# Attention and a gated FFN on one core: the last group's output projection as seven block products, with all tasks in a new order

## The chip, the cores and the metric

One Trainium2 chip; the kernel uses one of its cores. The metric is the device time of one execution in microseconds (us), less is better. Three timed runs of the kernel before took 246.59, 245.79 and 246.05 us; the median is 246.05 us.

The engines are named as in the profile: PE (TensorE, matrix products; PEld is its weight load), DVE (VectorE), ACT (ScalarE), POOL (GpSimd) and SP (SyncE, which here only issues DMAs). Each has its own queue of instructions, in program order, and waits on semaphores for the others.

## The reference

Causal attention over 4 batches, 8 heads, 768 positions and 64 elements per head; heads 0, 2 and 6 see all earlier positions, the others only the first 4 and the last 64. The result, 3072 tokens by 512, goes through a gated FFN of width 1536.

```python
scores = np.where(mask, q @ k.T / 8, -1e9)        # per batch and head
a = softmax(scores) @ v
x = a.transpose(0, 2, 1, 3).reshape(3072, 512)
g = x @ w_gate
return ((g * sigmoid(g)) * (x @ w_val)) @ w_out
```

## The kernel before

The 24 tiles of 128 tokens are taken in pairs. For each pair q, k and v are loaded, cast to 16 bits and turned (by PE for the first five pairs, by DMA after that). For each tile, score products go to PSUM (L567), ACT takes the exponential (L579), DVE or POOL multiplies masks in (L587), PE forms the values (L597), and DVE divides by the sum (L604, L605). The normalized tile is turned into `xt`, for the first eight tiles by PE and after that by a DMA transpose that SP issues (L615).

Four tiles make a group of 512 tokens, six groups in all. For each group `g` and each of twelve column blocks `j`, there are two blocks of four matmuls of 512 columns: the gate product and the value product (both L759; tasks `gate g.j` and `vals g.j`). ACT takes a tanh of the first (L765), DVE makes `sil` of it (`stt1`, L769), and DVE multiplies by the second into `h_sb` (`stt2`, L775).

The output projection is `h` times `w_out`. For groups 0 to 4 it is done as seven products of half blocks (`seventh`, L839; tasks `out g.p1` to `out g.p7`, 12 matmuls of 256 columns each) in place of eight. Their operands are partly sums of blocks of `w_out` (`ws`, made once, L412), partly sums of blocks of `h` (`hs g.x.part`, L826, on DVE or POOL; `x` 1 to 4, two parts each, one after the other: 1, then 3, then 2, then 4). Sums 2 wait for product 1, which reads the block that they overwrite, and sums 4 for product 2. Product 1 needs the lower half of `h`, products 2 and 4 the upper, product 5 sums 1, product 7 sums 3, product 6 sums 2, product 3 sums 4. The seven results are gathered in `out_sb` (`gathered`, L855, tasks `oe g.name`): `r1` is a copy, the others add a product to a cell. Cells c11, c12, c21 and c22 are the four quarters of the group's result; c12 adds product 3 to r56, which adds product 5 to r67. Two halves of 512 KB are stored per group.

Group 5, the last, is projected directly: per tile twelve matmuls of 512 columns (the last tile 384 and 128), 60 in all (`outproj`, L793). ACT copies the results out, DVE the last 128 columns, and each tile is stored as soon as it is there (L811); the last stores are of 192 and 64 KB.

PSUM has eight banks. Gates, products and scores take a bank each (scores two), and a bank is free when the operation that reads it is done.

The order is not found at run time. Three strings of digits hold it: `ORDER` gives all tasks in one sequence (numbers of 3700 and up are short runs of filling matmuls), `WAYS` the engine for each task that may go to several, `SLOTS` the bank or buffer for each task that takes one. Each engine runs its tasks in the order of that sequence.

Of the kernel before, what the change touches and what calls it, by code (L numbers as in the profile page):

```python
# [7 lines left out]
FP = mybir.dt.float32  # L8
# [8 lines left out]
    "0306071W091U1V1X000A08xy1c0D0C01050B1d1e040gy01f1gzJ1i1h2021282922232B1j1r1s021p1q1w0F2C2D2E2F1b"  # L17
    "2A2L2M2N2O2X2f2g0m1Y1a1Z1t1u1v1k0h252h1l1m2W2c242G2H2I2d2e2l2m2i2j0G271n1o1y1z3C262P2Q2R0z2t3031"
    "2J0y8e8o2n2K102U2o2p3I3J2V8t8j8m8u8v8k8l8n1x2k8f8g8p8q2x382y8h8i118r8s8w8x138y8z9893909495999A33"
    "340n9D9E0E2Z3K3D3L3M3N149B9C9F969G9H972a9192322b2Y2q2r2s2u3R3S3W3X0k1C9c9d9e9h9i9j3U3V3O2z353P36"  # L20
    "39370q1D9f9g9k9l3T3b3i3n3o3f3g0H3H3E3F2v2w0i169I9J9K9N9O9P0o179L9Q9R9M0l1F3Q3Y3Z3c3j3a0I3u40410j"
    "193k3h9m9n9o3l3m3A3B9S9T9U9r9s9t3d3e9X0J3v4344453G3p3q3r0r1G9u9p9v429Y9Z3s3t0x1H2S4647494A4H0p1A"
    "9V9WB74N4O4Q4R0K3z9q9zA10N4c3x4BB4B5B6B8Ak4K4L4V4b4C4D3yAT484M0w0sAQARASAU9a9b9y0t1E0W6K2TAlAmAV"
    "AWAX151M1O1N1PAYAZBEAfAgAhB9BABB4a0u181Q1R1SBCBDAp0v1BBFBGA0AaAbAnAoAc3wBHBIAdAe0L0M0PB20T12A41I"
    "1J1K0S4d4P0O4Z4h4g4Y4e4f5D5L5K0RAzB0B1AqArB31L0YALAM0ZAN4E4F4G4J4I6J1TAuAvAOAPAw9wA2A69xA3A7A55C"
    "5I5JAA4l4m4i4j4kACA8A9ABAD4n4v51524y53AiAj5f5lAEBMAGAFAK4S4z504T4W4UAxAy5g5nAsAtBL4q4r4o4p54BO0c"
    "AHAIAJ4s554t4u4x4wBJBKBQ56575T5U6MBNBP5W5c5XBb5j0X58595A5B707S7T6xBVBW6wBRBS5i5VBXBYBc6z5YBZBaBd"
    "5p5qBT5s605t5u4XBsBtBuCeCbCcCdCfCMCNCOCCBvBwCDCE0V6I5v0Q5F5G5H6v5k5o5M5N5O0UBiBjBk5rCPCQBlBm5E5Z"
    "5a5b5d5wCHCICJCWCXCY5m63696A666768Bh5h73CKCLC7C8C9710eCRCS5P5Q5R6465CACBCTBUC2C36y7Q6P74BnBo5x5y"
    "5z610a72CZCaBp5S625e6H6NBqBrC46B6C6F6D6GCFCGCiBeBfBgBxByBz7O7UC0C1C5C681CUCVCjCl6E6U6V6W6X6Y6R6S"  # L30
    "6T6eDmDjDkDlDnDoDpDqDrDs0b7P7X7WDtDuDv6Z6aCgChCn6b6c6d6fDUDVDWDXDY7576776g7C7D7E7F7G7L0dDwDxCkCm"
    "DSDFDGDHDPDQDRDT7b7c7d6QDADBDCDyDzE0DDDE7H80D5D6D7CsCt6O6n6o6h6i6j6kE1E27V7I7J7M7K7ND8D96l6m7879"
    "7A7BCoCpCrCuCv897Y7Z6p6q8786DKDLDMDZDaDb6L6r6s6t6uDcDdDeDfDgCwCx7e7f7R7j7m7n7o7p7q7rDNDOCyCzD0D4"
    "EhEiEjErEsEcEd88EkElEtCqD1D2D3EuEvEeDhDi7a7g7h7k7iFLFMFNFOFP7x8D8E8A8I8B8C8F8JFJFGFHFIFKFBFCFDDI"
    "DJE5E77s7t8GFEFFEp7u7v7y7w8HEXEYEZ0f838485EmEnEoEqEfEg8NEw8Y8ZE6E88T8U8VEzExEyF0EBE3E9E4EAECEDF6"
    "828K8L8M8OF1F2F3F9EFEG8Q8R8S8W8XEVEHEIEJF7F8FA7l8P7z8a8b8cEaEbESETEUEWEEEOELEM8dGiGMGTGUEKGCENER"
    "G7GVGWGjGkGJGKEPGREQFTFVGXGLGOGPGEGFGNGQG9F4GAGSGGGYGbGZF5GaGcGBGDFSGHFpFqFrFQFRG4G5GdGeFzFUFeFW"
    "FXGIG6G0G8FcFdGfFfFuFvFYFaFbGgGhG1G2G3FsFtFxGlGmFZFwFyFlFiFjFmFnFgFhFkFoGnGoGpGsGtGuGvGwGqGrGxGy"
    "GzH0H2H3H4H5H7H1H6H8H9"
)  # L40
WAYS = (
    "000010000000000000000000000000000000000000000000000000000000221202202202212200200111000111110010"
    "222200001100000000000000220022122022001011000000000000001100212002000011001001000001000001001000"
    "000201021120001000001001000000010010000010000000002221220000000000010000002000100100000020000221"
    "000000000100000002000010010000000000020200000010000000000000110000011000000100100000020001000000"
    "002202200220000000000000000012000100100000000201120000000000000000010002202202010000001001000001"
    "200000000000011002021000000000000000000200000000000000000000000000000000000000000000000000000000"
    "000000000000000000000000000000000000000000001000000000000000000000000000000000000000000000000000"
    "000000000000000000000000000000001000000010000000000000000000000000000000000000000000000000000000"
    "000000000000000000001110100011000000000001000000000000000000000000000000000000000000000000000000"  # L50
    "000000001111000001100000000000100000000000000000000000000000000000000000000000000000000000000111"
    "101100110000000000011000000000000000000000000000000000000000000000000000000000000000010000100000"
    "00000010"
)
SLOTS = (
    "0014237653916A152371476981504A39A2564807049A28352A9168410016041002241601230163620442561014104122"
    "636011642065221025144416322211256461406003404624344620616540610143626540604164236062324342142254"
    "041614064616325426212246140636104325614261306242452460436460636014122636230644521206164434062601"
    "020211341120003102001134000210400214105510131201001011040122021303213020111113411111040020200051"
    "014110101310002114301212131010022102320210013012111032112010000012000102211130011112010111054125"  # L60
# [959 lines left out]
```

## Time and profile before

| what | us |
| --- | --- |
| three timed runs | 245.79, 246.05, 246.59 |
| span of the profiled execution, first to last instruction | 244.4 |
| busy: PE, DVE, ACT, POOL | 234.5, 186.7, 148.5, 129.0 |
| first matmul starts | 1.4 |
| last matmul starts, last copy ends | 241.2, 241.8 |

The profile is of one more execution. Its span runs from the first to the last instruction; of its own whole time only the span is recorded, and the three timed runs lie 1.4 to 2.2 us above it. The profile lists instructions with start and length; the chain of work that ended last is followed back from the last instruction through what released each step. Idle time of an engine that nobody waits for costs nothing.

### The profile page before, as it was taken

To read this page: it belongs to the slowest core of one execution; us is meant where nothing else is said; L and a number is where in the kernel's file an instruction comes from. 1 tells how busy PE (TensorE), PEld (TensorE's weight loads), DVE (VectorE), ACT (ScalarE), POOL (GpSimd) and SP (SyncE) were. 2 spreads that over 40 slices of the span, in tenths; PEclk is the share of its full clock that TensorE was granted. 3 is DMA by queue.
4 is the path that set the end of the run, shared out by engine and by line. 5 is a ranking of instruction groups with operands and counts; after the bars stand their busy time and mean duration, and the time that the engine had idled before them with its cause. 6 is when DMAs were issued, how large, how long until landed. Compare 5 with 4: busy or idle time off the path is not lost.

```text
span 244.4 us, 5604 instructions
## 1 busy us (share of the span) xinstructions
PE 234.5 (96%) x2189; PEld 143.6 (59%) x2189; DVE 186.7 (76%) x324; ACT 148.5 (61%) x235; POOL 129.0 (53%) x140
## 2 busy tenths in 40 slices
PE   7989999998999999799999999999999999999995
PEld 3667855553457678445555457656456764475743
DVE  0577887889999999887987977669769777776800
ACT  3899899887878669487637776563682302330011
POOL 7479999956497552375765446910094110375000
PEclk9999999999999999999999999999999999999999
DMA  6999999999766989999464451519100213100053
GB/s 187 355 348 353 323 352 366 313 362 305 206 131 78 287 165 289 191 268 192 89 130 130 97 120 38 90 36 234 38 4 0 46 21 115 59 0 1 7 203 136
DMA packets 66794, 40.73 MB, mean 167 GB/s; under 512 B 25168, under 2 KB 60240, under 8 KB 66768
## 3 DMA queue, kind: packets, MB, share of 16 engines
q1 hardware_dynamic: 65392, 37.76, 61.5%
q10 hardware_dynamic: 1376, 2.62, 2.9%
q8 instruction: 17, 0.28, 0.5%
q14 instruction: 9, 0.07, 0.1%
HBM read 28.31 MB, written 6.29 MB: 142 GB/s over the span
## 4 chain that ended last, share of the span: by engine, by line
PE 54%; DVE 19%; issue 8%; DMA 6%; POOL 5%; SPq 5%; ACT 2%; DVEq 0%; POOLq 0%
PE banks L759 34%; PE banks L839 10%; PE banks L793 4%; DMA raw<-in_moe_w_val_dram 4%; DVE h_sb L775 4%; PE banks L567 3%; DVE h_sb L826 3%; SPq L349 3%; DVE sil L769 3%; PE banks L597 2%; POOL hs_sb L826 2%; DVE out_sb L855 2%; DVE xb L605 2%; DMA xt<-xb 2%; DVE e L587 2%
## 5 line engine op out<-in xcount | busy, mean ns | idle before, releaser
L759 PE MATMUL banks<-xt,wg_sb 128*128 128x512 f16 (+1 forms) x304 | 70.3, 368 | 1.9 <-DMA xt<-xb 1.4
L759 PE MATMUL banks<-xt,wv_sb 128*128 128x512 f16 (+1 forms) x304 | 70.4, 368 | 0.8 <-DVE sil L769 0.7
L579 ACT ACTIVATE e<-banks 128x1024 f16<-128x1024 f32 (+2 forms) x68 | 58.7, 910 | 20.0 <-PE banks L567 11.7
L765 ACT ACTIVATE sig<-banks 128x512 f32<-128x512 f32 (+1 forms) x76 | 43.0, 577 | 43.5 <-PE banks L759 37.5
L769 DVE SCALAR_TENSOR_TENSOR sil<-sig,banks 128x512 f32<-128x512 f32 (+1 forms) x76 | 49.0, 656 | 14.8 <-ACT sig L765 12.6
L775 DVE SCALAR_TENSOR_TENSOR h_sb<-sil,banks 128x512 f16<-128x512 f32 (+1 forms) x76 | 48.7, 656 | 6.7 <-PE banks L759 4.4
L587 POOL TENSOR_TENSOR e<-e,m 128x640 f16<-128x640 f16 (+1 forms) x22 | 37.8, 1727 | 27.2 <-ACT e L579 24.3
L759 PEld LDWEIGHTS <-wg_sb 128*128 128x128 f16 x304 | 28.5, 98 | 30.7 <-issue 3.1
L759 PEld LDWEIGHTS <-wv_sb 128*128 128x128 f16 x304 | 28.2, 98 | 29.5 <-issue 1.2
L839 PEld LDWEIGHTS <-h_sb 128*128 128x128 f16 x360 | 34.8, 98 | 7.9 <-issue 0.7
L826 POOL TENSOR_TENSOR hs_sb<-h_sb 128x768 f16<-128x768 f16 x7 | 11.5, 1640 | 40.9 <-DVE h_sb L775 29.4
L855 DVE TENSOR_TENSOR out_sb<-banks,out_sb 128x512 f32<-128x512 f32 x35 | 23.6, 685 | 4.7 <-PE banks L839 4.4
L826 POOL TENSOR_TENSOR h_sb<-h_sb 128x768 f16<-128x768 f16 x11 | 18.0, 1639 | 8.2 <-PE banks L839 4.4
L839 PE MATMUL banks<-wo_sb,h_sb 128*128 128x256 f16 x180 | 21.9, 273 | 0.0
L839 PE MATMUL banks<-wt_sb,h_sb 128*128 128x256 f16 x180 | 21.5, 273 | 0.4 <-DVE out_sb L855 0.4
L567 PE MATMUL banks<-qT,kT 64*128 64x128 f16 x472 | 20.6, 218 | 1.1 <-DVE xb L605 1.0
L567 PEld LDWEIGHTS <-kT 64*128 64x128 f16 x472 | 14.6, 94 | 11.0 <-issue 10.2
L597 PEld LDWEIGHTS <-e 128*128 128x128 f16 x472 | 17.1, 97 | 4.3 <-ACT vt L206 0.9
L597 PE MATMUL banks<-vt,e 128*128 128x65 f16 x472 | 18.2, 193 | 1.0 <-POOL vt L208 0.7
L605 DVE TENSOR_TENSOR xb<-banks,rc 128x512 f16<-128x512 f32 x24 | 16.6, 691 | 0.8
L208 POOL CAST vt<-raw 64x512 f16<-64x512 f32 x22 | 14.4, 654 | 4.8 <-DMA raw<-in_v_dram 2.3
L206 ACT COPY out_sb<-banks 128x512 f32<-128x512 f32 (+1 forms) x7 | 4.0, 570 | 19.1 <-PE banks L793 16.0
(60 smaller groups left out, 216.3 us busy)
## 6 DMA issues: line engine op xcount, KB each, us to landing
raw<-in_v_dram SPq DMA_DIRECT2D x12, 512.0 KB, 7.0
raw<-in_q_dram SPq DMA_DIRECT2D x8, 512.0 KB, 4.8
raw<-in_k_dram SPq DMA_DIRECT2D x8, 512.0 KB, 5.1
raw<-in_moe_w_gate_dram SPq DMA_DIRECT2D x6, 512.0 KB, 8.9
raw<-in_moe_w_val_dram SPq DMA_DIRECT2D x6, 512.0 KB, 8.4
raw<-in_moe_w_out_dram SPq DMA_DIRECT2D x6, 512.0 KB, 7.9
out_dram<-out_sb SPq DMA_DIRECT2D x6, 512.0 KB, 4.7
raw<-in_q_dram SPq DMA_DIRECT2D x8, 256.0 KB, 6.4
```

The source lines that it names most:

```text
L567: nc.tensor.matmul(sc[:, c:c + n, :], weights, moving, start=first, stop=last)
L579: nc.scalar.activation(out=to, in_=src, func=AF.Exp, scale=scale)
L587: ENG[task().way].tensor_tensor(out=ev, in0=ev, in1=mm, op=ALU.mult)
L597: nc.tensor.matmul(avs[t][:, odd, n * 66:n * 66 + 65], ee, vv, start=(m == 0), stop=(m == len(bl) - 1))
L605: nc.vector.tensor_tensor(out=xb.rearrange("p n o d -> p o n d"), in0=av[:, :, :, 0:64], in1=rc.to_broadcast([128, 2, 4, 64]), op=ALU.mult)
L759: nc.tensor.matmul(ps, wsb[:, kk, j * 128:(j + 1) * 128], xt[:, kk, c[0]:c[1]], start=(kk == 0), stop=(kk == 3))
L765: nc.scalar.activation(out=sg[g, j, c], in_=gs[g, j, c], func=AF.Tanh, scale=0.5)
L769: nc.vector.scalar_tensor_tensor(out=sl[g, j, c], in0=sg.pop((g, j, c)), scalar=1.0, op0=ALU.add, in1=gs.pop((g, j, c)), op1=ALU.mult)
L775: nc.vector.scalar_tensor_tensor(out=hs[g, j][:, c[0]:c[1]], in0=sl.pop((g, j, c)), scalar=0.5, op0=ALU.mult, in1=vs.pop((g, j, c)), op1=A ...
L826: ENG[T_hs[g, x][part].way].tensor_tensor(out=to, in0=a, in1=b, op=op)
L839: nc.tensor.matmul(rooms[g, p][:, x], left[:, j, 128 * x:128 * x + 128], right[:, j], start=(j == 0), stop=(j == NK - 1))
L855: nc.vector.tensor_tensor(out=cell(*to), in0=rooms[g, p], in1=cell(*other), op=ALU.add)
```

## The change

`SEVENS` goes from 5 to 6, so that group 5 is projected by seven products too. Its product 3, whose result is only needed for cell c12, is made in two halves of one token tile each (`p3.0` and `p3.1`, six matmuls each), each with a bank of its own; c12 is gathered by two additions of 256 columns, and stored as two DMAs of 128 KB. The other three quarters are stored by themselves, with 256 KB each (`store_cell`). All three strings are new, so every task of the kernel may stand elsewhere, on another engine or in another bank. The number of filling matmuls stays 21.

```diff
 ORDER = (
-    "0306071W091U1V1X000A08xy1c0D0C01050B1d1e040gy01f1gzJ1i1h2021282922232B1j1r1s021p1q1w0F2C2D2E2F1b"
...
+    "070006xi03090A0804021W1X0D011fy11U1V0C1g1c0B20211d280g1h1i1e222305292B1j0F1r2C1b1p1s2D0m1Y2A2E1q"
...
-    SEVENS = 5
+    SEVENS = 6
...
-    def seventh(g, p):
+    def halves(g, p):
+        return 2 if g == NG - 1 and p == 3 else 1
+
+    def seventh(g, p, part):
...
-        rooms[g, p] = buf("o", [128, 2, HM], FP, "o_ps")
-        for x in range(2):
+        if halves(g, p) == 1:
+            room = rooms[g, p] = buf("o", [128, 2, HM], FP, "o_ps")
+        else:
+            room = rooms[g, p, part] = buf("o", [128, 1, HM], FP, "o_ps")
+        for n, x in enumerate(range(2) if halves(g, p) == 1 else [part]):
             for j in range(NK):
                 nc.tensor.matmul(
-                    rooms[g, p][:, x], left[:, j, 128 * x:128 * x + 128], right[:, j],
+                    room[:, n], left[:, j, 128 * x:128 * x + 128], right[:, j],
                     start=(j == 0), stop=(j == NK - 1))
...
+        if halves(g, p) == 2:
+            nc.vector.tensor_tensor(
+                out=cell(*to)[:, part:part + 1], in0=rooms[g, p, part],
+                in1=cell(*other)[:, part:part + 1], op=ALU.add)
+            return
...
+    def store_cell(g, name, part):
+        x, y = CELLS[name][1]
+        b, i = TILES[FIRST[g] + 2 * x]
+        r0 = b * S + i * 128
+        at = slice(0, 2) if part is None else slice(part, part + 1)
+        eng = nc.scalar if T_st[g, name, part].way == "ACT" else nc.sync
+        eng.dma_start(
+            out=out[r0 + 128 * at.start:r0 + 128 * at.stop, HM * y:HM * y + HM].rearrange(
+                "(s p) n -> p s n", p=128),
+            in_=cell(x, y)[:, at])
...
+        if g == NG - 1:
+            ends = [("c11", None, c11), ("c21", None, c21), ("c22", None, c22)]
+            for part in range(2):
+                p3 = product(3, T_hs[g, 4] + wo, ["o"], part)
+                c12 = gather("c12", [p3, r56], part)
+                P.uses(p3, "o", c12)
+                ends.append(("c12", part, c12))
+            for name, part, done in ends:
+                st = T_st[g, name, part] = P.add(
+                    f"st{g}.{name}" + ("" if part is None else f".{part}"), ["SP", "ACT"],
+                    (lambda name=name, part=part: store_cell(g, name, part)), deps=[done])
+                P.lands(st)
+            return
```

Three places of the new order, each before and after. In these rows L839 and L855 of before are L845 and L866 of after.

DVE at the end of the program, before: the last `stt2` (L775), four gathering additions of group 4, and the copy of the last 128 columns.

```order
L769 SCALAR_TENSOR_TENSOR sil<-sig,banks 128x512
L775 SCALAR_TENSOR_TENSOR h_sb<-sil,banks 128x512
L855 TENSOR_TENSOR out_sb<-banks,out_sb 128x2x256 x4
L208 COPY out_sb<-banks 128x128
```

DVE at the same place, after: from the last `stt1` on, with the sums of group 5 (L826).

```order
L769 SCALAR_TENSOR_TENSOR sil<-sig,banks 128x512
L775 SCALAR_TENSOR_TENSOR h_sb<-sil,banks 128x512
L826 TENSOR_TENSOR hs_sb<-h_sb 128x768
L775 SCALAR_TENSOR_TENSOR h_sb<-sil,banks 128x512 x2
L866 TENSOR_TENSOR out_sb<-banks,out_sb 128x2x256 x2
L826 TENSOR_TENSOR h_sb<-h_sb 128x3x256
L826 TENSOR_TENSOR h_sb<-hs_sb,h_sb 128x3x256 x2
L866 TENSOR_TENSOR out_sb<-banks,out_sb 128x2x256 x6
L859 TENSOR_TENSOR out_sb<-banks,out_sb 128x256 x2
```

Behind the last `stt2` there were four additions and a copy; now there are two additions of group 4, three sums, and eight additions of group 5, in the order c11, r6, r67, c21, c22, r56, c12 first half, c12 second half. POOL, which had nothing of group 5, now makes four of its eight sums: part 0 of sums 3, then part 1 of sums 1, then both parts of sums 4 (part 1 first). On PE the new end is `out4.p4`, then products 2, 1, 7, 6, 4, 5 and the two halves of 3 of group 5.

SP at the end of the program, before: a store of group 3's second half (L861), then three stores of group 5.

```order
L861 DMA out_dram<-out_sb 128x2x512
L811 DMA out_dram<-out_sb 128x512
L811 DMA out_dram<-out_sb 128x384
L811 DMA out_dram<-out_sb 128x128
```

SP at the same place, after.

```order
L883 DMA out_dram<-out_sb 128x2x512 x3
L874 DMA out_dram<-out_sb 128x2x256 x2
L874 DMA out_dram<-out_sb 128x256 x2
```

Both halves of group 4 are now stored from SP (they were on ACT), and behind them c11, c21 and the two halves of c12; c22 is stored from ACT.

PE between the values of tile 11 (L597, the last of group 2's tiles to be ready) and the first gate of group 2 (L759), before: 48 matmuls of four products of group 1 (L839), then 16 of scores (L567); of each run only the first or last rows are shown.

```order
L597 MATMUL banks<-vt_110,e 128x65
L839 LDWEIGHTS h_sb
...
L839 MATMUL banks<-wt_sb,h_sb 128x256
L567 LDWEIGHTS kT_104
...
L567 MATMUL banks<-qT_107,kT_104 128x128
L759 LDWEIGHTS wg_sb
L759 MATMUL banks<-xt,wg_sb 128x512
```

PE at the same place, after: the scores (16 matmuls) stand behind the first product, and 11 more of scores (8 of tile 12, 3 of tile 14) behind the third.

```order
L597 MATMUL banks<-vt_110,e 128x65
L845 LDWEIGHTS h_sb
...
L567 MATMUL banks<-qT_107,kT_104 128x128
L845 LDWEIGHTS h_sb
...
L567 MATMUL banks<-qT_106,kT_104 128x128
L567 LDWEIGHTS kT_104
L567 MATMUL banks<-qT_107,kT_104 128x128
L845 LDWEIGHTS hs_sb
...
L845 MATMUL banks<-wt_sb,hs_sb 128x256
L759 LDWEIGHTS wg_sb
```

Four products still lie between the two, in the order 7, 6, 4, 5 in place of 6, 2, 7, 4 (product 2 stands ahead of tile 11's values now, and product 5 behind them), and the scores in two runs in place of one.

More of the change, by code (lines that the diff above doesn't have):

```diff
@@ L22 @@
[L22 to L36, printed above, removed]
@@ L869, in tasks_of_sevens, with product @@
         upper = [y for j in range(NK, NJ) for y in T_h[j]]
-        def product(p, deps, takes=(), after=()):
-            T_p[g, p] = P.add(f"out{g}.p{p}", ["PE"], (lambda: seventh(g, p)),
-                              deps=deps, takes=takes, after=after)
+        def product(p, deps, takes=(), part=None):
+            T_p[g, p] = P.add(f"out{g}.p{p}" + ("" if part is None else f".{part}"), ["PE"],
+                              (lambda: seventh(g, p, part)), deps=deps, takes=takes)
             return T_p[g, p]
@@ L881, in sums, with gather @@
                     (lambda part=part: hsum(g, x, part)), deps=deps(part)))
-        def gather(name, deps):
+        def gather(name, deps, part=None):
             T_ga[g, name] = P.add(
-                f"oe{g}.{name}", ["DVE"] if CELLS[name][2] else ["ACT", "DVE"],
-                (lambda: gathered(g, name)), deps=deps)
+                f"oe{g}.{name}" + ("" if part is None else f".{part}"),
+                ["DVE"] if CELLS[name][2] else ["ACT", "DVE"],
+                (lambda: gathered(g, name, part)), deps=deps)
             return T_ga[g, name]
```

69 lines of the change are left out of this document (42 added, 27 removed).

## The prediction

> **What bounds the kernel now.** I read the page first, then the chain of work that ended last, then the busy time by stretches.
>
> ```profile
> span 244.4 us, 5604 instructions
> PE 234.5 (96%) x2189; PEld 143.6 (59%) x2189; DVE 186.7 (76%) x324; ACT 148.5 (61%) x235; POOL 129.0 (53%) x140
> ```
>
> PE is busy for 96% of the span; the next engine, DVE, for 76%. A modelled PE share hides small waits, so the chain matters more. Its columns are start, length, engine and line, and a count of merged instructions.
>
> ```profile
> 95.85 0.50 SPq L615
> 96.40 4.70 DMA xt<-xb
> 101.24 5.34 PE banks L759 x24
> ...
> 136.75 0.85 PE banks L567 x24
> ...
> 141.15 0.33 PE banks L567 x8
> ...
> 197.62 2.62 PE banks L839 x24
> 200.24 13.81 PE banks L759 x64
> 214.05 1.31 PE banks L839 x12
> ...
> 227.06 3.93 PE banks L839 x36
> 230.99 10.40 PE banks L793 x60
> 241.47 0.29 DVE out_sb L208
> ```
>
> From 195 us to 241.4 us the chain is PE alone, each piece starting where the one before ends: there the kernel is bound by PE's work and by nothing else. Before that PE loses time here and there; the largest hole, 101.24, waits for a DMA. Three stretches show the other engines beside it (length, then PE, PEld, DVE, ACT and POOL busy, with counts).
>
> ```profile
> 60.00:100.00 40.00, 39.16 (x406) 27.35 (x404) 38.92 (x66) 29.84 (x44) 21.32 (x19) 1.00 0.90 188
> 100.00:196.00 96.00, 93.37 (x874) 54.83 (x875) 76.22 (x130) 57.42 (x91) 47.82 (x42) 1.00 0.52 107
> 196.00:241.50 45.50, 45.38 (x276) 26.31 (x274) 27.60 (x44) 9.88 (x17) 11.40 (x7) 1.00 0.19 67
> ```
>
> DVE is full from 60 to 100 us (38.92 of 40), and has 18 us free in the last 45.5. PE's granted clock is 1.00 in all three, so it enters no term.
>
> The sum is made against this execution: 244.4 us of span, to which the three timed runs add 1.4 to 2.2 us and their median 246.05 adds 1.65. I carry differences over to the median unchanged.
>
> **The change, part by part.**
>
> *Projection of the last group.* 60 matmuls of line 793 took 10.40 us. In their place stand 84 of 256 columns; twelve of those took 1.31 us (214.05), so 84 take 9.17 us. **-1.23 us**, all on PE at a place where only PE counts.
>
> *The end behind the last matmul.* In the new order, DVE has c22 and r56 (both from product 5), then the two halves of c12, behind the last products.
>
> ```profile
> 220.41 1.03 PE L759 MATMUL banks<-xt,wg_sb 128*128 128x512 f16 x4
> ...
> 220.61 0.69 DVE L855 TENSOR_TENSOR out_sb<-banks,out_sb 128x512 f32<-128x512 f32 x1 [2.06 <-PE banks L839]
> ...
> 224.44 0.69 DVE L769 SCALAR_TENSOR_TENSOR sil<-sig,banks 128x512 f32<-128x512 f32 x1
> 225.23 1.29 DVE L775 SCALAR_TENSOR_TENSOR h_sb<-sil,banks 128x512 f16<-128x512 f32 x2
> ```
>
> Here PE turns to its next task at 220.41 and DVE starts at 220.61: 0.20 us from PE to DVE. Two operations that don't need each other take 1.29 us together and 0.69 each: spacing 0.60. One that needs the result just written follows after 0.79 (224.44 to 225.23).
>
> ```profile
> L769 DVE SCALAR_TENSOR_TENSOR sil<-sig,banks 128x256 f32<-128x256 f32 x8 | 3.1, 419 | 1.7 <-ACT sig L765 1.5
> ```
>
> A half cell of 256 columns is not in this trace as an addition; the nearest row has 0.42 us, and the ends are 0.29 (128 columns, at 241.47) and 0.69 (512). I take 0.42. With E the end of PE: product 5 ends at E-1.31, c22 starts at E-1.11, r56 at E-0.51, c12's first half (it reads r56) at E+0.28, the second 0.34 later, and ends at **E+1.04**. Before, the copy starts at 241.47, 0.20 behind PE, and ends at E+0.49. So **+0.55 us**.
>
> *The last store* grows from 64 KB to 128.
>
> ```profile
> out_dram<-out_sb SPq DMA_DIRECT2D x1, 192.0 KB, 1.9
> out_dram<-out_sb SPq DMA_DIRECT2D x1, 64.0 KB, 1.6
> ```
>
> Between 1.6 and 1.9 us: **+0.15 us**, ends 0 and 0.3. The three earlier quarters issue while PE still works or 0.3 us ahead of it; they cost nothing unless SP's queue holds the last one up.
>
> *Does PE stay fed until E?* What hid waits at the end was 10.4 us of work that needed only h. Now products 7, 6 and 3 wait for sums, and these for the last stt2. I follow the new order by hand from group 4's gate 8 on. To the end of the last gate product PE has 27 blocks of 0.86 us and 7 products of 1.31: 32.5 us. DVE has 40 full operations and 8 sums in it.
>
> ```profile
> 203.50 1.28 DVE L769 SCALAR_TENSOR_TENSOR sil<-sig,banks 128x512 f32<-128x512 f32 x2 [1.21 <-ACT sig L765]
> 204.70 0.68 DVE L855 TENSOR_TENSOR out_sb<-banks,out_sb 128x512 f32<-128x512 f32 x1
> 205.30 0.55 DVE L826 TENSOR_TENSOR h_sb<-h_sb 128x768 f16<-128x768 f16 x1
> 205.76 0.68 DVE L775 SCALAR_TENSOR_TENSOR h_sb<-sil,banks 128x512 f16<-128x512 f32 x1
> ```
>
> At 0.60 each, and 0.46 for a sum (205.30 to 205.76), that is 27.7 us: DVE keeps up, with 4.8 us to spare. The last stt2 starts 0.55 us behind the last gate product. During out4.p4, p2 and p1 (3.9 us) the chain behind it runs: stt2 0.69, the sum on POOL 1.64, the next on DVE 0.55; product 7 finds its operand 0.2 us early. The two sums behind p1 (0.20 + 0.46 + 0.55) are ready 0.1 us before product 7's 1.31 us are over. So no wait, by a hair: **0**, with an upper end of 1.8 that the rivals price.
>
> *The replanning.* DVE's work moves with it: between tile 3's normalization and tile 23's the new order gives DVE 225 tasks, the old one 232, though DVE's total grows from 291 to 316. That is relief where DVE is full and load where it has 18 us free. Two terms can be read from the order. First, group 2's first gate.
>
> ```profile
> 93.08 1.01 PE L597 MATMUL banks<-vt,e 128*128 128x65 f16 x28
> 93.92 1.47 PE L839 MATMUL banks<-wt_sb,h_sb 128*128 128x256 f16 x12
> ...
> 99.25 0.62 PE L567 MATMUL banks<-qT,kT 64*128 64x128 f16 x16
> 101.24 1.02 PE L759 MATMUL banks<-xt,wg_sb 128*128 128x512 f16 x4 [1.36 <-DMA xt<-xb]
> ```
>
> Tile 11's values end at 93.9; its normalized rows must be transposed by DMA before the gate, which starts at 101.24. PE fills the time with four products and 16 score matmuls, and then stands for 1.36 to 1.5 us. In the new order 11 more score matmuls (0.033 each, from 0.85 for 24 and 0.33 for 8) and one more turn to scores lie there: **-0.6 us**; ends 0 (the DMA lands later by as much) and -1.5. Second, such turns.
>
> ```profile
> 179.99 1.03 PE L759 MATMUL banks<-xt,wg_sb 128*128 128x512 f16 x4
> 180.95 0.62 PE L567 MATMUL banks<-qT,kT 64*128 64x128 f16 x14
> ```
>
> Four matmuls at 0.216 end at 180.85, the scores start at 180.95: 0.10 lost, and 0.07 more in the run itself (0.33 less 8 times 0.033). The 68 score tasks stand in 32 runs before, in 29 now: 3 times 0.17, **-0.5 us**, ends 0 and -0.6. Against these I set one new wait that I can't see, of the size of this one, **+0.45 us**:
>
> ```profile
> 188.95 1.47 PE L839 MATMUL banks<-wt_sb,h_sb 128*128 128x256 f16 x12 [0.45 <-DVE out_sb L855]
> ```
>
> Its ends are wide. Down, all that PE idles from 60 to 196 us in the rows above (40.00 less 39.16 and 96.00 less 93.37, 3.5 us) beside the 1.36 already counted: -2.1. Up, a handful of such new ones. The first 56 us, where loads bind, keep the order of the first twelve loads but for the first two; 0.
>
> **Sum:** -1.23 + 0.55 + 0.15 + 0 - 0.6 - 0.5 + 0.45 = -1.18; span 243.2, time **244.9 us**.
>
> **The rivals.**
>
> *DVE comes late at the end (slower).* The point is the mean spacing: 40 operations at 0.70 and 8 sums at 0.56 fill PE's 32.5 us. Gates wait for banks that DVE frees, so from there on PE waits. By hand at these spacings, the last gate product waits 0.5 us for its bank, product 2 another 0.5, product 6 0.8: 1.8 us. Each 0.01 us more adds 0.4. Without the -0.6 of the transposes, whose landing may move as well, 244.9 + 1.8 + 0.6 is **247.3 us**. For it: dependent pairs do take 0.79. Against: few pairs in the new order are dependent. 0.22.
>
> *A sum loses the port to POOL (no change).*
>
> ```profile
> 183.35 0.56 DVE L826 TENSOR_TENSOR h_sb<-h_sb 128x768 f16<-128x768 f16 x1 [0.81 <-POOL hs_sb L826]
> ...
> 186.25 1.64 POOL L826 TENSOR_TENSOR h_sb<-h_sb 128x768 f16<-128x768 f16 x1 [2.93 <-DVE h_sb L826]
> ...
> 186.68 1.61 DVE L826 TENSOR_TENSOR h_sb<-hs_sb,h_sb 128x768 f16<-128x768 f16 x1
> ```
>
> A sum on DVE takes 0.56 alone; begun inside one of POOL's it took 1.61 and ended 0.40 behind it. At the end, hs5.2.0 on DVE and hs5.4.1 on POOL come free within 0.1 us of each other, and product 6 waits for the first. If POOL wins, POOL's 1.64 and the 0.40 behind it end 1.6 us after product 7, and the time is **246.5 us**. Against: DVE's is queued directly behind hs5.2.1, for which POOL must still wait. 0.22, with the cases in which gains and new waits cancel. The Trainium skill (SBUF — State Buffer, "Who interferes with whom") says that a DVE instruction with two SBUF inputs and a GpSimd one that reads SBUF exclude each other, and that issue order decides; these rows agree, and by it DVE, being first, would lose nothing.
>
> *The replan closes the other old waits too (faster still).* -2.1 more: **242.8 us**. For it: DVE's lighter middle. Against: many of the old waits are a chain's length, not a load. 0.12.
>
> *My forecast*: 0.44, with a range of its own of 244.0 to 245.3.
>
> **How the numbers follow.** A measurement of this kernel can tell 0.3%, 0.74 us, from no change. Forecast and the faster rival lie below 245.3: 0.56. Port and cancellation: 0.22 within. Late DVE: 0.22 slower. The range runs from the faster rival to the slower, 242.8 to 247.3.
>
> **What would show it.** PE's last group: 84 matmuls in about 9.2 us, without holes, the first one right behind out4.p4; DVE ending about 1.0 us behind PE; the wait before group 2's first gate near 0.9 us; fewer gaps around scores. Holes before products 2, 7 or 6, with DVE busy, would make me wrong at the end; new PE waits of 0.5 us or more between 60 and 195 us, in the middle.

## The result, and the profile after

| | us, median (lowest to highest) | runs |
| --- | --- | --- |
| before, beside it | 245.95 (245.79 to 246.59) | 4 |
| after | 242.58 (242.52 to 243.07) | 4 |

The ratio is 0.9868, with a 95% interval of 0.9851 to 0.9885: 3.4 us less. The profiled execution took 242.56 us, with a span of 240.8 against 244.4 before. The forecast was 1.2 us less (244.9); its range ended at 242.8, 0.2 us above the result.

The page after: span, then busy time of each engine, its share and its instructions.

```profile
span 240.8 us, 5648 instructions
PE 233.4 (97%) x2213; PEld 147.1 (61%) x2213; DVE 199.0 (83%) x346; ACT 139.9 (58%) x223; POOL 125.1 (52%) x142
```

PE is busy 1.1 us less, though the span fell by 3.6: PE does less, and also waits less. By stretches (length, then PE, PEld, DVE, ACT and POOL busy with counts, granted clock, DMA share, GB/s):

```profile
60.00:100.00 40.00, 38.79 (x412) 27.06 (x410) 37.01 (x60) 28.22 (x44) 29.17 (x26) 1.00 1.00 206
100.00:196.00 96.00, 96.00 (x887) 56.95 (x886) 76.66 (x133) 55.59 (x91) 45.92 (x42) 1.00 0.51 101
196.00:240.80 44.80, 40.97 (x279) 27.05 (x277) 35.74 (x60) 7.69 (x13) 6.73 (x4) 0.98 0.20 71
```

From 100 to 196 us PE was busy 93.37 of 96 us before, now all 96.00. DVE's 38.92 of 40 us between 60 and 100 fell to 37.01. In the chain of waits around group 2's first gate (100.43, L759) no DMA stands any more; PE's pieces follow each other:

```profile
93.72 1.48 PE banks L845 x12
95.20 0.55 PE banks L567 x16
95.76 2.73 PE banks L845 x24
...
98.51 0.51 PE banks L567 x11
99.02 1.42 PE banks L845 x12
100.43 0.86 PE banks L759 x4
```

The view of what PE waited for between 56 and 236 us (releaser, us in total, times, longest) has four lines before and one after:

```profile
PE banks L759 <- DMA xt<-xb: 1.4, 1, 1.4
PE banks L759 <- DVE sil L769: 1.1, 3, 0.4
PE banks L567 <- DVE xb L605: 1.0, 2, 0.5
PE banks L839 <- DVE out_sb L855: 0.6, 2, 0.4
```

```profile
PE banks L845 <- DVE h_sb L775: 1.0, 1, 1.0
```

To place the 3.6 us I took, in both traces, each matmul's distance to the next one's start less the pace of its kind (0.216 us for 512 columns, 0.109 for 256, some 0.035 for scores, 0.029 for values). What exceeds the pace is PE's loss, and a gap is a place where a single such loss is over 0.15 us.

| part of the span, us | before | after | difference | predicted |
| --- | --- | --- | --- | --- |
| matmuls at their pace | 223.78 | 222.50 | -1.28 | -1.23 |
| loss in single gaps over 0.15 us, behind 56 us | 5.86 | 2.06 | -3.80 | -0.15 |
| smaller gaps between tasks, behind 56 us | 3.59 | 4.12 | +0.53 | -0.5 |
| the rest: first 56 us, gaps within tasks | 6.58 | 6.65 | +0.07 | 0 |
| from the last matmul's start to the end | 3.2 | 4.1 | +0.9 | +0.70 |

In the second row the predicted -0.15 is the -0.6 at group 2's gate and the +0.45 for one new wait.

### The profile page after: what moved, and what is told of

Read it like the earlier page. It is cut to its first block, busy times and chain, and to the rows that moved or that the text cites. A ratio compares the mean times of both kernels' runs of the same rounds, so it can differ in the third digit from the quotient of the medians.

```text
span 240.8 us, 5648 instructions
## 1 busy us (share of the span) xinstructions
PE 233.4 (97%) x2213; PEld 147.1 (61%) x2213; DVE 199.0 (83%) x346; ACT 139.9 (58%) x223; POOL 125.1 (52%) x142
## 3 DMA queue, kind: packets, MB, share of 16 engines
q10 hardware_dynamic: 1632, 2.88, 3.3%
## 4 chain that ended last, share of the span: by engine, by line
PE 75%; DVE 16%; DMA 4%; issue 2%; ACT 1%; POOL 1%; SPq 0%; DVEq 0%; POOLq 0%; ACTq 0%
PE banks L759 45%; PE banks L845 15%; PE banks L567 7%; DVE out_sb L866 4%; PE banks L597 4%; PE banks L321 3%; DVE h_sb L775 3%; DMA raw<-in_k_dram 2%; PE banks L473 2%; DVE e L587 2%; DVE sil L769 2%; DVE xb L605 2%; DVE h_sb L826 2%; DMA out_dram<-out_sb 1%; DVE wt_sb L412 1%
## 5 line engine op out<-in xcount | busy, mean ns | idle before, releaser
L759 PE MATMUL banks<-xt,wv_sb 128*128 128x512 f16 (+1 forms) x304 | 71.6, 368 | 0.0
L759 PE MATMUL banks<-xt,wg_sb 128*128 128x512 f16 (+1 forms) x304 | 70.7, 368 | 0.3 <-DVE xt L208 0.2
L775 DVE SCALAR_TENSOR_TENSOR h_sb<-sil,banks 128x512 f16<-128x512 f32 (+1 forms) x76 | 48.8, 654 | 13.8 <-PE banks L759 12.7
L845 PEld LDWEIGHTS <-h_sb 128*128 128x128 f16 x432 | 41.5, 98 | 9.9 <-issue 1.1
L759 PEld LDWEIGHTS <-wg_sb 128*128 128x128 f16 x304 | 29.0, 98 | 29.3 <-issue 0.8
L759 PEld LDWEIGHTS <-wv_sb 128*128 128x128 f16 x304 | 27.8, 98 | 27.5 <-DVE wv_sb L212 0.2
L826 POOL TENSOR_TENSOR h_sb<-h_sb 128x768 f16<-128x768 f16 x10 | 16.8, 1689 | 52.8 <-PE banks L759 51.2
L866 DVE TENSOR_TENSOR out_sb<-banks,out_sb 128x512 f32<-128x512 f32 x41 | 27.7, 686 | 7.7 <-PE banks L845 4.5
L587 POOL TENSOR_TENSOR e<-e,m 128x1024 f16<-128x1024 f16 (+1 forms) x15 | 28.2, 1882 | 5.1 <-ACT e L579 4.9
L845 PE MATMUL banks<-wo_sb,h_sb 128*128 128x256 f16 x216 | 26.2, 273 | 1.0 <-DVE h_sb L775 1.0
L845 PE MATMUL banks<-wt_sb,h_sb 128*128 128x256 f16 x216 | 25.6, 273 | 0.0
L567 PE MATMUL banks<-qT,kT 64*128 64x128 f16 x472 | 20.4, 218 | 0.3
L597 PEld LDWEIGHTS <-e 128*128 128x128 f16 x472 | 17.7, 97 | 4.2 <-DVE e L587 0.4
L826 POOL TENSOR_TENSOR hs_sb<-h_sb 128x768 f16<-128x768 f16 x7 | 12.0, 1709 | 15.7 <-DVE h_sb L775 8.4
L567 PEld LDWEIGHTS <-kT 64*128 64x128 f16 x472 | 14.5, 94 | 8.8 <-issue 7.1
L597 PE MATMUL banks<-vt,e 128*128 128x65 f16 x472 | 18.9, 193 | 0.0
L587 DVE TENSOR_TENSOR e<-e,m 128x640 f16<-128x640 f16 (+1 forms) x23 | 17.5, 780 | 0.1
L208 POOL CAST hq<-raw 128x1024 f16<-128x1024 f32 (+1 forms) x12 | 11.6, 965 | 6.5 <-DMA raw<-in_q_dram 3.3
```

Of the source, the lines that this page charges most:

```text
L567: nc.tensor.matmul(sc[:, c:c + n, :], weights, moving, start=first, stop=last)
L587: ENG[task().way].tensor_tensor(out=ev, in0=ev, in1=mm, op=ALU.mult)
L597: nc.tensor.matmul(avs[t][:, odd, n * 66:n * 66 + 65], ee, vv, start=(m == 0), stop=(m == len(bl) - 1))
L759: nc.tensor.matmul(ps, wsb[:, kk, j * 128:(j + 1) * 128], xt[:, kk, c[0]:c[1]], start=(kk == 0), stop=(kk == 3))
L775: nc.vector.scalar_tensor_tensor(out=hs[g, j][:, c[0]:c[1]], in0=sl.pop((g, j, c)), scalar=0.5, op0=ALU.mult, in1=vs.pop((g, j, c)), op1=A ...
L826: ENG[T_hs[g, x][part].way].tensor_tensor(out=to, in0=a, in1=b, op=op)
```

## The experiments

In the diffs, lines are tasks in the order of one engine, with the names of the program. `sc`, `val`, `nm` and `xdma` are a tile's scores, values, normalization and transposing DMA, `mask` its multiplication by a mask; `cx` converts value rows, `load q` loads query rows and `dq` turns them; the first number is the tile, pair or group. Each ratio is to the kernel before, run beside it; so are differences, by the medians, where nothing else is said.

### Order alone, and seven products alone

The first run keeps the new order and projects group 5 directly. The second keeps the old order and the new kernel's code, with the seven products of group 5 and their sums put in at its end.

```diff
-    SEVENS = 6
+    SEVENS = 5
```

> The new order with group 5 projected directly again (60 matmuls, before's order for them at the end). Replan theory: of the 3.4 us gained, the order gives about 3 and the seven products 0.4 (1.28 us less PE work, 0.84 us longer end): 243.0 us, span 241.2, PE waits outside the pace of its matmuls still near 12.8 us. Projection theory: the seven products give most of it: 245 us or more.

> The old order, and the seven products of group 5 at its end (out4.p5 ahead of out4.p3, part 0 and 1 of the sums in changed roles because there the last stt2 belongs to part 0). Replan theory: 245.5 us, 0.4 less than before, with the old waits in the middle unchanged. Projection theory: 243.5 or less. If the end starves PE in this order: up to 246.5, with holes before product 7 or 6.

Order alone: 243.15 us (243.06 to 244.75), ratio 0.9908 [0.9875, 0.9940]: 3.0 of the 3.4 us by the medians (1.5 to 3.1 by the interval), with four of the five gaps after. The second took 249.09 us (248.46 to 249.45), ratio 1.0121 [1.0093, 1.0148]; missed. Its PE rows at the end show two new holes:

```profile
228.44 1.47 PE L845 MATMUL banks<-wt_sb,hs_sb 128*128 128x256 f16 x12 [0.78 <-DVE h_sb L775]
...
234.04 2.78 PE L845 MATMUL banks<-wo_sb,h_sb 128*128 128x256 f16 x24 [1.51 <-DVE out_sb L866]
```

Both are of my making: out4.p5 was put ahead, into the bank that the last `stt2` reads, and group 5's product 2 got the bank that out4.p5 is gathered from last. So this was no clean test, and a better joint was tried below.

### The old waits, one cause at a time

In the old order, PE's waits have a pattern. Around 188 us (DVE rows; the sum at 186.68 that took 1.61 us beside POOL's is in the prediction, as is PE's product that starts at 188.95 behind it):

```profile
188.22 0.68 DVE L855 TENSOR_TENSOR out_sb<-banks,out_sb 128x512 f32<-128x512 f32 x1
188.82 0.19 DVE L604 RECIPROCAL rc<-banks 128x8 f32<-128x8 f32 x1
```

The addition at 188.22 frees the bank that PE waits for; ahead of it in DVE's queue stands a sum that nobody needs yet, held by POOL. Such a sum or mask stood ahead of most of the waits over 0.15 us. So in the kernel before, six of them were moved behind the operation that PE waits for:

```diff
-hs0.3.1
 cx4.0.1
 stt1 1.9.0
+hs0.3.1
...
+stt1 1.1.0
 mask8.0
-stt1 1.1.0
...
-hs0.4.1
 oe0.c11
 mask10.0
 oe0.r6
+hs0.4.1
...
-hs1.3.1
 oe0.c12
 nm10
+hs1.3.1
...
+nm16
 hs2.2.1
-nm16
...
+oe3.c11
 hs3.2.1
-oe3.c11
```

> The old order and the old projection; only six places of DVE's order differ: hs0.3.1 behind stt1 1.9, mask8.0 behind stt1 1.1, hs0.4.1 behind oe0.r6, hs1.3.1 behind nm10, hs2.2.1 behind nm16, hs3.2.1 behind oe3.c11. Port theory: the eight PE waits of 0.28 to 0.67 us behind them (4.1 us in all) arose because DVE's work for PE was queued behind a sum or mask that waited for POOL's; most go, 2.5 to 4 us less: 242.5 to 243.5 us. Rival: these waits have other causes (load of the engines, choice of engine for masks and sums), and at most 0.8 us goes: 245.2 us or more.

245.03 us (243.68 to 245.79), ratio 0.9946 [0.9923, 0.9970]. Seven gaps of 0.17 to 0.67 us went, 3.3 us in all. Before, the six moved operations began beside one of POOL's and took 0.85 to 1.75 us; here they take 0.54 to 0.89, where a sum alone takes 0.55 and such a mask 0.68. Two old gaps stayed: the one at 59.60 fell from 0.42 to 0.18 us, and the one at 191.40 is still there (0.62). Directly ahead of the `stt1` that PE waits for there stand two copies of value rows and no sum; its cause was not tested. One gap of 0.90, behind an exponential, is new at 92 us.

But the gap at group 2's gate grew from 1.54 to 2.46 us: PE came earlier, and the gate started at 101.30 as before (101.24). Something else fixes that time. The last tile landed at 101.17, 0.13 us ahead of the gate (101.10 and 101.24 before). The profile puts this wait down to a DVE sum that ended at 101.29, but the gate reads nothing of it.

### Group 2's gate: cover, or an earlier landing?

First the prediction's step: the 11 score matmuls are taken from ahead of the gate in the new kernel.

```diff
 out1.p4
+out1.p5
+gate2.2.0
 sc12.0
 sc14.2
-out1.p5
-gate2.2.0
```

> The new kernel with 11 score matmuls (sc12.0 and sc14.2) behind group 2's first gate instead of ahead of it. By the prediction's step (the DMA lands when it did, and the 11 score matmuls with their turn are what filled 0.6 us of the wait) a wait of 0.5 to 0.6 us comes back before that gate: 243.1 us. Rival, that the transposed tiles land earlier in the new order than before, so that this work covers nothing: gate at about 99.6, no wait over 0.2 us, 242.5 to 242.7 us.

243.92 us (243.81 to 244.03), ratio 0.9898 [0.9874, 0.9922]: slower than both theories. Its chain (start, length):

```profile
97.47 2.48 DMA xt<-xb
...
100.08 1.02 PE banks L759 x4
101.11 0.35 PE banks L567 x8
...
101.48 1.03 ACT e L579
...
102.56 0.64 PE banks L597 x16
```

The last tile now lands at 99.95, where before it landed at 101.10; the gate waits 0.37 us. The rest is a wait of my own making: this kernel also has new banks for five tasks and a cast of key rows ahead of an exponential on ACT, and the values at 102.56 got a bank that the scores directly ahead of them hold until their exponential is done. So its time is no measure of the cover; but the landing moved by 1.15 us, which cover cannot explain.

What lies beside the transposes? Before, SP issued a load of 512 KB of query rows at 93.09, ahead of the two transposes; the new order issues its loads behind them. Landing times of the two, from their issue (first line before, second after):

```profile
DMA to landing us min/median/max: 4.7/5.1/5.5
```

```profile
DMA to landing us min/median/max: 2.5/3.2/4.0
```

Two edits of that one place, in the old order and, reversed, in the new one:

```diff
 xdma10
-load q9
 xdma11
 xdma9
+load q9
```

> The kernel before with one SP instruction moved: the 512 KB load of query rows that was issued at 93.09, behind the last two tile transposes ahead of group 2's first gate instead of ahead of them. Theory that this load, in flight beside them, is why the last tile landed at 101.1 in the trace before and at 99.95 in the run of the new order with less cover: landing by 100.0, the wait of 1.54 us falls to 0.4 or less, 244.9 to 245.2 us. Rival, that the landing follows from when the tiles are normalized and from their own two issues (95.15 to 98.43): gate at 101.2 as before, 246.0 us. Third case, the load's late rows are themselves waited for behind 105 us: 246 or more with a new hole there.

```diff
 dq6.0
+load q8
 xdma11
 xdma10
-load q8
```

> The new kernel with the reverse edit: its query load of 98.41 us issued ahead of the last two tile transposes. Theory that a load in flight beside them delays them: the last tile lands about 1.1 us later (near 101), TensorE arrives at 100.3 and waits 0.5 to 0.9 us: 243.1 to 243.5 us. Rival, that the landing does not depend on it: 242.6 us.

With the load behind: 245.81 us (244.98 to 246.08), ratio 0.9975 [0.9948, 1.0001], unclear; in the profile (an execution of 244.98) the span fell by 1.2. What the DMA engines did from 93 to 101 us (slices of 0.2 us, tenths busy), before:

```profile
DMA  9999999999999999999999990090007999003997
```

With the load behind, and the landing of the two transposes there:

```profile
DMA  9999999400000000599400099911016354599999
```

```profile
DMA to landing us min/median/max: 2.5/3.0/3.6
```

Before, the 16 DMA engines are full when the transposes are issued (95.15 and 96.40), until 97.8; here they are idle from 94.6 to 96.2. The last tile lands at 99.88 in place of 101.10, and the gate starts at 100.01. The 0.41 us that PE still waits there ends with a DVE mask, no longer with the DMA.

With the load ahead in the new kernel: 243.99 us (243.77 to 244.32), ratio 0.9900 [0.9842, 0.9958], 1.4 us above the new kernel. What PE waited for:

```profile
PE banks L759 <- DMA xt<-xb: 1.2, 1, 1.2
PE banks L845 <- DVE h_sb L775: 1.0, 1, 1.0
```

The wait is back, more than expected: the load itself waited for its buffer and held the transposes up on SP, the last one was issued at 97.98 (97.03 after) and landed at 101.55 (99.54 after). Of these 2.0 us the later issue is 0.95, the longer landing 1.06.

Then both causes together, the six moves on DVE and the load:

> The kernel before with the six sums and masks behind the awaited VectorE operations (the run that gave 245.0, where the wait at group 2's gate grew to 2.46 us) and the query load behind the two tile transposes. Theory of two causes, VectorE's in-order sums and this DMA: the gate at 99.4 to 100.0, 1.3 to 1.9 us off the earlier run: 243.3 to 243.7 us, nearly all that the new order gave. Rival, that the DMA is bound by its own issue: gate at 101.2, 245.0 us.

243.52 us (243.15 to 244.28), ratio 0.9875 [0.9805, 0.9944]; as the theory of two causes had it. By the medians the single effects are 1.1 and 0.4 us, the two together 2.7, but the intervals are too wide to show that they add to more than their sum. The traces show it at the gate: it starts at 101.24 before, at 101.30 with the moves alone, at 100.01 with the load alone and at 99.30 with both. While the tile lands late, the moves bring this gate nothing; once it lands early, 0.7 us. One edit did harm: with hs2.2.1 behind nm16, the sum ran beside POOL at 133.53 for 2.01 us and PE lost 1.30 us at 136 us, where it had lost 0.67; in the run of the moves alone the same sum took 0.55 there.

At 186 us it shows how a sum that stands behind does no harm:

```profile
185.44 0.69 DVE L866 TENSOR_TENSOR out_sb<-banks,out_sb 128x512 f32<-128x512 f32 x1
186.05 0.89 DVE L826 TENSOR_TENSOR h_sb<-hs_sb,h_sb 128x768 f16<-128x768 f16 x1
```

### Joints of the two orders

Three kernels take one order up to a point and the other behind it: the new one up to group 2's first gate and the old behind it, the reverse, and the old one up to group 4's first gates with the new one, seven products included, behind.

> The new order up to group 2's first gate, the old order behind it, group 5 projected directly as before. Theory that the waits are separate places, each closed by the order around it: TensorE's loss beyond its matmul pace up to that gate was 12.1 us in the trace before and 10.8 after, so the gain here is 1.3 us and the old waits behind it stay (0.67 near 137 us, 0.61 and 0.61 near 190): 244.7 us. Rival, that the order pays only as a whole, because a tile, a bank or a turn left late by one part is paid for in the other: new waits of 0.5 us or more appear behind the joint, 245.5 to 247.

> The old order up to group 2's first gate, the new order behind it, group 5 projected directly as before. Theory of separate places: the loss behind that gate was 3.9 us before and about 2.0 after, so the gain is 1.9 us, while the 1.54 us wait before the gate stays: 244.2 us; this and the other half add up to the 3.0 us that the whole order gave. Rival, that the order pays only as a whole: 245.5 to 247, the two gains adding to much less than 3.0.

> The old order up to the first gate products of group 4 (about 178 us), the new order from there on, with the seven products in group 5. Theory of separate places: 1.28 us less of matmuls, 0.8 more at the end behind them, and the two old waits of 0.61 near 190 us gone with some 0.2 of turns: 246.0 - 1.28 + 0.8 - 1.4 = 244.2 us, with no hole in group 5. Rival, that seven products at the end need more than the order of the last quarter (as the earlier run with the old order and holes before out4.p5 and out5.p2 may be read): holes in group 5 again, 246 or more.

All missed: 259.60 (1.0540 [1.0516, 1.0564]), 254.04 (1.0336 [1.0274, 1.0398]) and 253.98 us (1.0290 [1.0233, 1.0347]). Each joint leaves work that one order does late and the other wants early. In the first, DVE's queue:

```profile
109.21 1.38 DVE L212 TENSOR_REDUCE vt<-raw 64x512 f16<-64x512 f32 x2 [7.58 <-DMA raw<-in_v_dram]
110.51 2.00 DVE L866 TENSOR_TENSOR out_sb<-banks,out_sb 128x512 f32<-128x512 f32 x3
```

A conversion of value rows waits 7.58 us for a load issued late, the additions that free PE's banks stand behind it, and PE stands still for 10.5 us. So these runs can't say what each half of the order is worth. They show one thing beside the joint: the gaps over 0.15 us between 56 and 95 us are those of the order used there, to within 0.02 us, and past the joint's own holes the old order has its two at 190 us again (0.6 each, now at 202 and 205), while the new one has none in either of its two runs. The waits belong to the order of the rows around them.

A cleaner joint lies at 190 us, where the two orders have done the same tasks but a dozen, no load among them:

> The old order up to out3.p5 (about 190 us in the profile), the new one behind it, with the seven products in group 5. This joint is where the two orders have done nearly the same tasks, and no load differs; the earlier joints left tiles or loads out of place. Theory that the seven products are worth their matmuls less the longer end: 246.0 - 1.28 + 0.84 = 245.5 us, no hole in group 5. Rival, that they need the whole new order ahead of them (as the holes before out4.p5 and out5.p2 in the earlier run with the old order would have it): holes of 0.5 us or more again, 247.5 or more.

246.04 us (245.60 to 247.06), ratio 0.9989 [0.9963, 1.0015]: 0.2 us less, where 0.45 was expected, and unclear beside no change; 0.6 was the difference between the new order with and without the seven products. Group 5 has no gap over 0.15 us: it doesn't need the new order ahead of it. In the profiled execution, the slowest of ten, the matmuls take 1.29 us less, but what follows the last one's start takes 1.19 more (0.87 more in the new kernel).

### The named causes together

> The old order with the named edits alone: five sums and masks behind the awaited VectorE operations (the sixth, hs2.2.1, stays where it was, since moving it cost a wait of 1.30 us at 136 us where it saved 0.67), the query load behind the two tile transposes, and the end with the seven products from 190 us on. Theory that these causes are the gain: 243.5 less 0.6 less 0.2 to 0.45 gives 242.4 to 242.8 us, the time of the new kernel. Rival, that a good part of the gain is spread over the order: 243.5 or more.

243.09 us (242.56 to 244.81), ratio 0.9864 [0.9835, 0.9894], the new kernel's ratio (0.9868). The median lies between the two expectations, three of five executions are at 243.1 or below. The profiled one is the slowest of them, with two gaps of 1.24 us (at 97.36) and 1.39 us (at 104.17). DVE has the cause of both:

```profile
96.62 1.29 DVE L866 TENSOR_TENSOR out_sb<-banks,out_sb 128x512 f32<-128x512 f32 x2 [1.48 <-DMA out_dram<-out_sb]
```

```profile
101.47 1.67 DVE L826 TENSOR_TENSOR h_sb<-h_sb 128x768 f16<-128x768 f16 x1
```

The additions that free PE's bank waited for a store of group 0, which landed at 96.52, 7.1 us after its issue. Then another sum, hs1.4.0, ran beside a mask on POOL (101.33, 1.40 us), with an `stt1` behind it that PE waits for; this sum had taken 0.55 before. So its trace isn't a typical one. It shows that the same sum at the same place in DVE's order may or may not meet POOL, as what comes ahead of it shifts.

Five moved DVE operations, one moved load, and the new order with the seven products from 190 us on make up the change's gain, within the interval. They don't do it gap by gap: the old gaps at 136 us (0.66) and 190 us (0.62) are still there, which the new order doesn't have.

### What the new order still waits for

After, PE's longest gap is before out0.p2 at 72.20. POOL, DVE and PE there:

```profile
69.49 1.65 POOL L826 TENSOR_TENSOR h_sb<-hs_sb,h_sb 128x768 f16<-128x768 f16 x1 [0.16 <-PE banks L845]
```

```profile
69.84 1.71 DVE L826 TENSOR_TENSOR h_sb<-hs_sb,h_sb 128x768 f16<-128x768 f16 x1 [1.17 <-PE banks L845]
71.47 0.68 DVE L775 SCALAR_TENSOR_TENSOR h_sb<-sil,banks 128x512 f16<-128x512 f32 x1
```

```profile
72.20 1.47 PE L845 MATMUL banks<-wo_sb,h_sb 128*128 128x256 f16 x12 [1.03 <-DVE h_sb L775]
```

The two parts of one sum start 0.35 us apart on POOL and DVE; DVE's ends 0.4 us behind POOL's, and the `stt2` that PE waits for stands behind it.

```diff
-hs0.2.1
 stt2 1.11.0
+hs0.2.1
```

> The changed kernel; only hs0.2.1 on DVE stands behind stt2 1.11 and no longer ahead of it. Port theory: the largest wait that is left, 1.19 us before out0.p2 at 72 us, is that sum's wait for POOL's; it goes, and what carries to the end is between 0.65 us (what DVE gains) and 1.2: 241.4 to 241.9 us. Rival: the next waits take it back (the wait before group 2's first gate returns): 242.4 to 242.6.

242.14 us (242.03 to 243.31), ratio 0.9852 [0.9820, 0.9883]. The gap is gone; 0.32 opened at 73.67 and 0.51 at 113.34. Between the theories. The second of these waits for a transposing DMA of query rows, and a run below whose edit is at the end has it too (0.59 at 114.39), so it may belong to the execution and not to the edit. A second step moved the sum three places further on DVE, put vals2.8 ahead of sc16.0 on PE, and r56 ahead of c22 at the end (that diff is shown below):

```diff
-hs0.2.1
 stt1 1.4.0
 ws1.0
...
 stt2 1.5.0
+hs0.2.1
...
+vals2.8.0
 sc16.0
 sc16.3
-vals2.8.0
```

> The new kernel with the sum hs0.2.1 three places further behind on VectorE than in the run that gave 242.1, vals2.8 ahead of sc16.0 on TensorE, and r56 ahead of c22 at the end. Theory that each remaining wait goes by itself: 0.32 at vals1.4, 0.51 at sc16.0 and 0.2 at the end off 242.1: 241.2 us. Rival, that what is closed opens elsewhere, as in the earlier run, which gained 0.4 of the wait's 1.19: 241.8 to 242.3.

242.36 us (242.17 to 242.41), ratio 0.9847 [0.9823, 0.9872]: the rival, 0.06 above its upper end. What is closed opens in part elsewhere. Both are at the new kernel's time or a little below it (0.2 to 0.4 us), not clearly faster.

### The end

```diff
 oe5.c21
+oe5.r56
 oe5.c22
-oe5.r56
 oe5.c12.0
```

> The new kernel with r56 ahead of c22 on VectorE at the end, so that the first half of c12 follows an addition whose result it doesn't read. By the prediction's spacings (0.79 behind a result just written, 0.60 otherwise) the end moves 0.2 us forward: 242.4 us. Rival, that c12 waits for its own product, not for r56: no change at the end, 242.6.

243.31 us (242.62 to 244.60), ratio 0.9890 [0.9862, 0.9918], no gain; the profiled execution has a gap of 0.59 us at 114.39 that has nothing to do with the edit. In its trace c12's first half starts 0.21 us behind the last matmul's start (0.45 after), so DVE did gain the 0.2 us; what follows it took 0.3 us more. Inconclusive.

```diff
+oe5.c11
 hs5.2.0
-oe5.c11
```

> The new kernel with the sum hs5.2.0 behind c11 on VectorE, so that POOL's sum hs5.4.1 starts ahead of it. By the prediction's port rival the sum begins inside POOL's 1.64 us and ends 0.4 us behind it, product 6 stands 1.2 to 1.6 us: 243.8 to 244.2 us. Rival, that the sum's place costs only its own delay, since product 6 has 1.3 us of product 7 ahead of it: 242.6 to 243.0.

246.49 us (244.91 to 247.86), ratio 1.0013 [0.9986, 1.0040]: 3.9 us more than the new kernel, but not by the port. DVE and PE:

```profile
232.75 0.69 DVE L866 TENSOR_TENSOR out_sb<-banks,out_sb 128x512 f32<-128x512 f32 x1 [1.81 <-ACT out_sb L206]
233.35 0.55 DVE L826 TENSOR_TENSOR h_sb<-hs_sb,h_sb 128x768 f16<-128x768 f16 x1
```

```profile
233.96 2.25 PE L845 MATMUL banks<-wt_sb,h_sb 128*128 128x256 f16 x19 [2.31 <-DVE h_sb L826]
```

The sum takes its 0.55, as alone. It stands behind c11 now, c11 waits for ACT's copy r1, and r1 for the store of group 4 that still reads `out_sb`. The profiled execution (244.91) is the fastest of ten, and this wait accounts for all that it loses (span 243.1 us against 240.8). The five slowest (246.71 to 247.86) have a mean granted clock of 0.992 or 0.993, the other five 0.999 or 1.0; what they lose beyond that wait is in no trace. The price of a lost port at the end was not measured.

## Why the prediction was wrong, point by point

- **PE's last group** (-1.23): -1.28 of pace. Right.
- **The end behind the last matmul** (+0.55): DVE ends 1.10 us behind PE's end (1.04 forecast), and 0.55 behind it before, so +0.55. **The last store** (+0.15): from DVE's end to the end of the span 2.61 before, 2.88 after: +0.27. Right. What starts the last chain was not foreseen:

```profile
229.28 2.84 DMA out_dram<-out_sb
...
232.22 0.59 ACT out_sb L206
...
232.84 0.27 DVE out_sb L866
...
237.15 0.42 DVE out_sb L859
```

  The copy r1 waits for a store of group 4 to land at 232.12, and DVE then works without a pause to the end. This chain brings DVE to c22 at 235.75, and product 5 would have allowed 235.70: the two paths meet, so the sum came out right with one of its causes left out; the run with c11 ahead of the sum shows what a later store would cost.
- **PE stays fed until E** (0): right, no gap over 0.15 us behind 99 us. So the two slow rivals did not occur.
- **The replanning** (-0.65 in all) is the step that failed, and it was a mis-sized term: PE's losses fell by 3.2 us, mostly in old waits that the sum left as they were.
  - *Group 2's gate, -0.6*: -1.54, the lower end of its bounds. The forecast let the DMA land when it did and counted cover. Shown by the two moves of the load: the landing depends on a load issued ahead of the transposes on SP's queue. Cover was the smaller part: PE arrives 0.6 us later, the tile lands 1.56 us earlier (99.54 for 101.10).
  - *The other old waits, left as they were*: 4.3 us in gaps over 0.15 us, all gone. They were the rival of 242.8 us at 0.12, against which the prediction said that "many of the old waits are a chain's length, not a load". Seven of the nine, 3.3 us, were neither: a sum or mask stood ahead of the awaited operation in DVE's queue and ran late beside POOL, and moving six of them in the old order took these gaps away. One of the other two (0.61 at 191.40) stayed under these moves, and its cause is open. Prediction and rows had both halves of this, the port at 186.68 and the PE wait at 188.95, and did not join them.
  - *One new wait, +0.45*: 2.06 us in five gaps, the largest 1.19 by the same mechanism.
  - *Three fewer score runs, -0.5*: 0. A turn does cost 0.21 us (0.10 into the scores, 0.11 out, over 16 and 14 turns before), more than the 0.17 assumed; but the three runs that went lie in the first 56 us, where loads bind, and behind that there are 18 before and after. The smaller gaps grew by 0.53 because turns that lay inside longer waits before now stand by themselves: there were 30 by themselves before (16 in, 14 out), and are 35 after.
- **Port rival at the end**: did not occur; DVE's sum came first, as the prediction's row order said. Collisions elsewhere did not become fewer: some 11 DVE operations that read two SBUF tiles ran over a quarter longer than alone beside POOL in either trace. What changed is how often PE waits for what stands behind them. The Trainium skill (SBUF — State Buffer, "Who interferes with whom") states the exclusion; the rows at 69.49 and 69.84 agree, with 1.71 us for a sum that alone takes 0.55.

What stays open: how the gain of the order divides over its stretches, since each of the three joints brought holes of its own; the cause of the old gap at 191.40; and the cost of the lost port at the end. That the new order gains by the same causes as the edits of the old one is concluded from the waits that are gone and from the equal time.

## What to carry to other kernels

When PE waits for an in-order engine, look at what stands ahead of the awaited operation on that engine, and whether anybody needs it yet: moving it behind is often free, though not always (hs2.2.1 met POOL at its new place, and hs5.2.0 came behind an operation that waits for a store). Here six such moves and one moved load were worth 2.7 us of 246. Two causes that end at the same gate can hide each other: the moves brought group 2's gate forward by nothing alone, and by 0.7 us once the tile landed early. So an edit that gains little may be half of one that gains more. A small transfer that PE waits for is better issued ahead of a large load on the same queue than behind it: at this gate that was worth 1.2 us of landing in the old order.

## What the runs showed of the hardware

- The last two transposing DMAs of 128-token tiles ahead of group 2's gate take 2.5 to 4.2 us to land where the 512 KB load is issued behind them (the kernel after, and every run with that order of issue), and 3.6 to 6.3 us where it is issued ahead of them. There each of them landed 0.5 to 2.0 us behind the load (before: load 99.34, tiles 100.62 and 101.10). The Trainium skill (DMA: Bandwidth & Descriptors, "Queues, rings and completion order") says that what one engine issues goes into one ring on each of the DMA engines and is taken in ring order; the landings agree: between 88 and 106 us what SP issued landed in the order of issue in each of the 18 traces.
- After long holes PE's clock is halved. In the first joint, with PE idle from 102.0 to 112.6 us (length, PE busy, granted clock, DMA share, GB/s):

```profile
112.50:114.50 2.00, 1.94 (x5) 0.50 0.53 194
114.50:116.50 2.00, 2.00 (x6) 0.50 0.93 189
116.50:118.50 2.00, 2.00 (x10) 0.83 0.51 86
```

  So the hole cost 2.3 us more: some 4.7 us at half pace. A hole of 5.9 us did the same, and so did three of 1.9, 1.2 and 0.5 us within 4.8 us; single holes of 2.3 and 2.5 us did not in the executions that were profiled. The Trainium skill (TensorE: Matmul & The Clock Gate, "What's actually happening") gives a window of about 3.4 us without work; the three holes show that idle time in pieces may do.
- In the run with c11 ahead of the sum, executions of one kernel lie 3 us apart, and the slower half has a mean granted clock 0.006 to 0.008 lower. Half pace for 3 to 4 us would do that to the mean (an estimate from the 244 us of the span), as behind the holes above; no trace of a slower one was kept.
